# Turning the first two pairs of B·x as plain halves (ScalarE and accumulating transfers), with the fourth chunk's sum of v on the tensor engine

## The chip, the cores and the metric

The kernel runs on one core of a Trainium2 chip. Its time is the device time of one execution in microseconds; runs are summarized by their median. In the text PE is the tensor engine (matmuls), PEld its loading of weights, DVE the vector engine, ACT the scalar engine, POOL GpSimd and SP the sync engine, which issues most transfers.

## The reference

Two branches over a sequence of 2048 rows with 1024 channels, mixed by a gate for each row. Branch a is a diagonal state space model with 1024 complex states; branch b is a short convolution, a product and a long convolution (by FFT) for each channel.

```python
g = sigmoid((x * gate_w).sum(-1, keepdims=True))

# a: h_t = Lam_bar * h_(t-1) + B_bar x_t, complex
Lam_bar = exp(dt * Lam)
B_bar = ((Lam_bar - 1.0) / Lam)[:, None] * Bmat
Bu = einsum("bld,pd->blp", x, B_bar)
h = Lam_bar * h + Bu[:, t]            # for each t
a = 2.0 * einsum("blp,dp->bld", hseq, Cmat).real + x * Dskip

# b: taps of k, times v, long convolution with ssm_k
k_shift = sum over t of k_pad[:, t:t + S] * shift_k[:, 3 - t]
kv = k_shift * v
y = irfft(rfft(kv, 2 S) * rfft(ssm_k, 2 S))[:, :S] + kv * ssm_D
b = x * y

return g * a + (1 - g) * b
```

## The kernel before

**Branch b** is the convolution stage, up to about 210 us. It takes the channels in eight chunks of 128. The FFT is a product with cosine and sine tables (`CF`, `SF`, `NCF` forwards, `CI`, `SI` backwards) on PE. One pass of the main loop, `for c in range(NC - 1)` (lines 1186 to 1312), works on several chunks at once: on DVE the products of the spectra of chunk c (`products`: `acc<-BT,Vh`, `wkh<-BT,Vh` and the sums behind them, at the end `Vh<-acc`); on PE the inverse of chunk c−1 (`inverse`, `psz`, evicted to `cv`), the forward transforms of chunk n = c+1 (`fwd_K`, `psk`, evicted into `BT`; `fwd_V`, `psv`, evicted into `Vh`), and the taps of chunk c+2. ACT evicts nearly all of these. The products of a chunk need all four `Vh` evictions of `fwd_V`, which stand at the end of the pass before.

Before `fwd_V`, the product kv of the chunk has to be folded into two halves (`times_v`, lines 601 to 615): DVE multiplies `ks` by v; PE mirrors `ks` with a reversal matrix (`mirror`), ACT evicts that to `lo`; DVE takes the difference `ev = ks − lo`, and the sum `ks + lo` is made in place by an accumulating transfer issued by GpSimd (`ks<-lo`, the helper `gather`, line 126). The call for chunk c in `times_v(c)` runs in the pass before the one of its products: `times_v(3)` is stepped in pass c=2.

**Branch a** takes time in four blocks of 512 steps (`tb`) and the states in eight groups (`g`) of two times 128, and each pair (tb, g) has two parts j of 128 states. A block's columns are taken in two halves, even and odd steps, and two steps are joined to one: what has to be scanned is V(t) = even(t) + Lam_bar·odd(t−1), complex; this is called turning. `Bu(i)` (lines 833 to 861) makes the i-th pair of `order`. Before the change there are two ways to turn:

- `Bu_tile` (863 to 884), for i = 0 and 1, which are (tb 0, g 0) and (tb 0, g 1): `odd` is evicted to `U`; then PE adds Lam_bar·odd into the PSUM tile `even` by matmuls with diagonal matrices (`even<-U,lamd`, four for each part), and ACT evicts the turned `even`. The diagonals `lamd` are made by `lam_diag` (820 to 831): for g 0 by six scalings on ACT (line 1248), for g 1 by six on DVE at the end of pass c=1 (line 1311).
- `Bu_halves` (888 to 904, i = 2 and 3) and `Bu_plain` (906 to 920, later ones): `even` and `odd` are evicted plainly, into `V_` and `O_`, and `turn_U` (922 to 936) does the rest, in two steps. Step 1: two ACT scalings of 512 columns, `O_` by the real part of lam, into a buffer `Q`, and an accumulating transfer of 256 KB, `U<-Q`. Step 2: four scalings of 256 columns by the imaginary part and its negative, and another such transfer.

The parts of the first four pairs are stepped in between the work of the convolution, at places chosen by hand (`step(parts)`); the turns of pairs 2 and 3 run at lines 1254 and 1364. The scans over the turned pairs (`scan`) and the products with C (`psy`) follow the convolution, from about 208 us to the end.

**The order of the work.** Nothing is reordered: `put` (line 86 and on) chains every instruction behind the one issued before on the same engine, so the order in which the Python code runs is the order on each engine, GpSimd's and SP's queues too. All PSUM tiles come from one pool of four buffers in rotation (`ps2`), so each new tile waits for the eviction of the fourth one before it. `u4` is a pool of three buffers, for `hr`, `t` and `Q`.

All operations go through these helpers, so the trace names the helper's line (L94), and instructions are told apart by their tiles.

## Time and profile before

| | us |
|---|---|
| median of 3 runs (lowest, highest) | 380.2 (378.99, 381.24) |
| the profiled execution | 381.04 |
| its span in the trace | 379.3 |

| engine | busy us | share of the span | instructions |
|---|---|---|---|
| PE | 369.9 | 98% | 2434 |
| PEld | 200.3 | 53% | 2469 |
| DVE | 364.1 | 96% | 585 |
| ACT | 307.6 | 81% | 473 |
| POOL | 79.1 | 21% | 109 |

The span is the time from the first instruction to the last in the trace, the profiled execution's own time lies 1.7 us above it. Busy is the time in which an engine worked on at least one instruction. In the timeline a row has the start, the duration, the engine, the operation with its output and inputs and their shapes, a count when several of one kind follow each other, and in brackets the time for which the engine stood idle ahead of it and what ended that. Since matmuls are pipelined, the duration of one is longer than the step from it to the next.

### The profile page before, as it was taken

What the parts mean: (1) busy time and instruction counts of PE and PEld (TensorE: products, weight loads), DVE (VectorE), ACT (ScalarE), POOL (GpSimd) and SP (SyncE); (2) the same over time, 40 slices, a digit from 0 to 9 for tenths busy, and PEclk for the clock granted to TensorE, in tenths of its full rate; (3) what the DMA queues carried; (4) which work ended last, traced back from release to release, by engine and by line L of the source; (5) the groups of instructions that cost most, each with busy time, mean ns of one, the idle gap of its engine ahead of it and who ended that gap; (6) DMA issues with size and microseconds to landing.
All of it is one profiled execution on the core that took longest, in us unless ns stands there. A gap on an engine that the chain in (4) does not pass through costs nothing.

```text
span 379.3 us, 6647 instructions
## 1 busy us (share of the span) xinstructions
PE 369.9 (98%) x2434; PEld 200.3 (53%) x2469; DVE 364.1 (96%) x585; ACT 307.6 (81%) x473; POOL 79.1 (21%) x109
## 2 busy tenths in 40 slices
PE   7999999999999999999999999989999999999996
PEld 4656467575674847644544444434445444444444
DVE  8899999999999999999999999999999989969984
ACT  5879998988979899697949799998879868938501
POOL 4011030110301102021002012123443313635000
PEclk9999999999999999999999999999999999999999
DMA  7889999999999989968999999947998999998902
GB/s 168 168 114 264 215 213 189 236 218 203 228 200 185 215 166 194 179 145 153 207 183 209 215 186 253 256 101 131 197 247 138 251 247 204 160 255 146 221 0 111
DMA packets 126259, 71.78 MB, mean 189 GB/s; under 512 B 104649, under 2 KB 107601, under 8 KB 126226
## 3 DMA queue, kind: packets, MB, share of 16 engines
q1 hardware_dynamic: 112416, 45.90, 56.1%
q0 software_dynamic: 12688, 25.17, 38.7%
q10 hardware_dynamic: 1122, 0.28, 0.4%
q8 instruction: 19, 0.31, 0.3%
q14 instruction: 14, 0.11, 0.1%
HBM read 15.48 MB, written 8.39 MB: 63 GB/s over the span
## 4 chain that ended last, share of the span: by engine, by line
DVE 55%; PE 26%; issue 8%; DMA 5%; ACT 4%; POOL 0%; SPq 0%; POOLq 0%; DVEq 0%
PE psy L94 23%; DVE acc L94 20%; DVE wkh L94 13%; DVE A L94 5%; DVE Vh L94 4%; DVE t L94 3%; DVE U L94 2%; DVE ks L94 2%; DMA U<-Q 2%; ACT Q L94 2%; DVE trn L94 2%; PE taps L94 1%; DMA kT<-in_B_k_dram 1%; DMA BT<-gd 1%; DVE CT L94 1%
## 5 line engine op out<-in xcount | busy, mean ns | idle before, releaser
L94 PE MATMUL psy<-CT,U 128*128 128x512 bf16 (+1 forms) x418 | 92.7, 374 | 0.4
L94 PEld LDWEIGHTS <-U 128*128 128x128 bf16 x492 | 48.0, 98 | 57.3 <-issue 2.1
L94 PEld LDWEIGHTS <-BT 128*128 128x128 bf16 x544 | 50.5, 98 | 33.5 <-issue 0.2
L94 DVE TENSOR_TENSOR wkh<-BT,Vh 128x2048 bf16<-128x2048 bf16 (+3 forms) x31 | 44.6, 1457 | 0.0
L94 ACT ACTIVATE Q<-U,lam 128x512 bf16<-128x512 bf16 (+1 forms) x64 | 37.5, 632 | 8.5 <-DVE U L94 8.5
L94 POOL DMA_DIRECT2D U<-Q x26 | 26.6, 1033 | 82.9 <-ACT Q L94 42.4
L94 DVE TENSOR_TENSOR acc<-BT,Vh 128x4096 bf16<-128x4096 bf16 (+3 forms) x19 | 36.9, 1947 | 0.3 <-ACT Vh L94 0.2
L94 PE MATMUL both<-xT,BT 128*128 128x512 bf16 x157 | 35.2, 379 | 0.2
L94 ACT ACTIVATE Vh<-psv 128x1024 bf16<-128x1024 f32 x32 | 30.7, 1034 | 5.7 <-PE psv L94 5.6
L94 DVE TENSOR_TENSOR_SCAN A<-rv,init,A 128x256 bf16<-128x256 f32 x48 | 34.4, 738 | 0.0
L94 DVE TENSOR_TENSOR acc<-acc,wkh 128x1024 bf16<-128x1024 bf16 (+4 forms) x30 | 32.7, 1128 | 0.1
L94 ACT ACTIVATE U<-both 128x512 bf16<-128x512 f32 x44 | 24.2, 594 | 10.4 <-PE both L94 10.1
L94 ACT ACTIVATE BT<-psk 128x1024 bf16<-128x1024 f32 x31 | 30.0, 1035 | 2.3 <-PE psk L94 2.2
L94 POOL DMA_DIRECT2D acc<-wkh x8 | 9.7, 1218 | 100.7 <-DVE wkh L94 100.7
L94 PE MATMUL psk<-eok,SF 128*128 128x384 bf16 (+1 forms) x118 | 28.0, 354 | 0.2
L94 PEld LDWEIGHTS <-SF 128*128 128x128 bf16 x184 | 18.0, 98 | 19.1 <-issue 0.4
L94 PE MATMUL psz<-Vh,CI 128*128 128x512 bf16 x64 | 24.3, 379 | 0.0
L94 PE MATMUL psz<-Vh,SI 128*128 128x512 bf16 x64 | 24.3, 379 | 0.0
L94 PE MATMUL taps<-dg,kT 128*128 128x128 bf16 (+1 forms) x352 | 21.5, 208 | 1.0 <-DMA kT<-in_B_k_dram 1.0
L94 PEld LDWEIGHTS <-kT 128*128 128x128 bf16 x352 | 20.8, 99 | 2.5 <-DMA kT<-in_B_k_dram 2.0
L94 DVE TENSOR_TENSOR U<-U,trn 128x512 bf16<-128x512 bf16 (+1 forms) x58 | 21.2, 391 | 0.1
L94 PE MATMUL both<-xT,BTl 128*128 128x512 bf16 x94 | 21.1, 379 | 0.1
(223 smaller groups left out, 767.5 us busy)
## 6 DMA issues: line engine op xcount, KB each, us to landing
U<-Q POOLq DMA_DIRECT2D x26, 256.0 KB, 5.4
acc<-wkh POOLq DMA_DIRECT2D x6, 768.0 KB, 8.7
cv_scr<-cv SPq DMA_DIRECT2D x16, 256.0 KB, 4.8
kn<-in_B_ssm_k_dram SPq DMA_DIRECT2D x5, 512.0 KB, 3.7
v<-in_B_v_dram SPq DMA_DIRECT2D x5, 512.0 KB, 5.9
out_dram<-m SPq DMA_DIRECT2D x8, 256.0 KB, 4.8
BT<-cv_scr SPq DMA_DIRECT2D x7, 256.0 KB, 7.0
out_dram<-BT SPq DMA_DIRECT2D x7, 256.0 KB, 2.0
```

The lines of the kernel that those rows point to most:

```text
L94: i = f(*a, **kw)
```

## The change

The first two pairs are made as the later ones: `Bu_tile` and `lam_diag` go, and pairs 0 and 1 use `Bu_halves`, with `even` and `odd` evicted plainly. Their turns (`turn_U`) run in the passes c=4 (pair 0) and c=5 (pair 1): step 1 behind `fwd_K`, step 2 between the first two and the last two tiles of `fwd_V`. The column before the first step of the first block is set to zero by a small ACT operation (`before_first`). So per pair six ACT scalings and two accumulating transfers of 256 KB come in, and the matmuls with diagonals and the twelve scalings that make the diagonals go.

Besides, the difference `ev = ks − lo` of chunk 3 (stepped in pass c=2) is no longer made by DVE but by PE, in a PSUM tile `whole`: the identity times the upper half of `ks`, plus `refl[:, 0]`, the reversal matrix with the other sign, times the lower; four matmuls of 512 columns, and an ACT eviction.

```diff
@@ kernel's pools
+    s5p["Q"] = s5p["wu"]
...
@@ times_v(c)
         e = eo_pool.tile([128, 2, 4, 128], BF16, name="ev")
-        tt(e, ks[:, 2:4], lo, ALU.subtract)
+        if c == 3:
+            ps = ps2([128, 2, 4, 128], "whole")
+            for mt in range(2):
+                mm(ps[:, mt], ident, ks[:, 2 + mt], True, False)
+                mm(ps[:, mt], refl[:, 0], ks[:, 1 - mt], False, True)
+            act(e, ps, func=ACT.Copy)
+        else:
+            tt(e, ks[:, 2:4], lo, ALU.subtract)
...
-    def lam_diag(g, home, on_act=False):
...
@@ Bu(i)
-        if i >= 2:
-            V_, O_ = U[:, 0:4 * HB], U[:, 4 * HB:]
...
-        U = U[:, 0:8 * HB].rearrange("p (a c j t) -> p a c j t", a=2, c=2, j=2)
-        Us[tb, g] = U[:, 0], U[:, 1]
-        return [Bu_tile(tb, g, U, j) for j in range(2)]
-
-    def Bu_tile(tb, g, U, j):
...
+        V_, O_ = U[:, 0:4 * HB], U[:, 4 * HB:]
+        V_ = V_.rearrange("p (c j t) -> p c j t", c=2, j=2)
+        O_ = O_.rearrange("p (c j t) -> p c j t", c=2, j=2)
+        Us[tb, g] = V_, O_[:, :, :, 2:]
+        turns_U[i] = turn_U(g, V_, O_)
+        return [(Bu_halves if i < 4 else Bu_plain)(tb, g, V_, O_, j) for j in range(2)]
...
+    def before_first(tb, g, O_, j):
+        if j == 0 and tb > 0:
+            act(O_[:, :, :, 1], ends[:, 1 - tb % 2, g], func=ACT.Copy)
+        elif j == 0:
+            act(O_[:, :, :, 1], lam[:, :, 0:2], func=ACT.Copy, scale=0.0)
...
@@ for c in range(NC - 1)
         fwd_K(n, (2, 3))
-        if c == 1:
-            lam_diag(0, lam_pool, True)
         if c == 4:
             step(parts)
+        if c in (4, 5):
+            step(turns_U[c - 4])
         if c == 6:
             run(sp)
-            s5p["Q"] = s5p["wu"]
             run(turns_U[2])
...
         fwd_V(n, (0, 1))
+        if c in (4, 5):
+            run(turns_U[c - 4])
         if c < 6 and c != 4:
             step(parts)
...
         fwd_V(n, (2, 3))
         if c in (4, 5):
             step(parts)
-        if c == 1:
-            lam_diag(1, lam_pool)
```

More of the change, by code (lines that the diff above doesn't have):

```diff
@@ L408 @@
     mlam = small("mlam")
-    lamd = {}
     TCS = rot_pool.tile([128, 2, NP, HB], BF16, name="TCS")
@@ L818 @@
     ends = consts.tile([128, 2, NG, 2, 2], BF16, name="ends")
-    def lam_diag(g, home, on_act=False):
-        if g == 0:
-            lamd["all"] = home.tile([128, 2, 2, 3, 128], BF16, name="lamd", tag="lamd")
-        t = lamd[g] = lamd["all"][:, g]
-        for j in range(2):
-            for k, f in enumerate((lam[:, 0], lam[:, 1], mlam)):
-                pi = 2 * g + j
-                if on_act:
-                    act(t[:, j, k], ident, func=ACT.Identity, scale=f[:, pi:pi + 1])
-                else:
-                    ts(t[:, j, k], ident, f[:, pi:pi + 1], None, ALU.mult)
     def Bu(i):
@@ L851, in Bu @@
                 U = home.tile(shape, BF16, name="U")
-        if i >= 2:
-            V_, O_ = U[:, 0:4 * HB], U[:, 4 * HB:]
-            V_ = V_.rearrange("p (c j t) -> p c j t", c=2, j=2)
-            O_ = O_.rearrange("p (c j t) -> p c j t", c=2, j=2)
-            Us[tb, g] = V_, O_[:, :, :, 2:]
-            turns_U[i] = turn_U(g, V_, O_)
-            return [(Bu_halves if i < 4 else Bu_plain)(tb, g, V_, O_, j) for j in range(2)]
-        U = U[:, 0:8 * HB].rearrange("p (a c j t) -> p a c j t", a=2, c=2, j=2)
@@ L860, in Bu @@
-        Us[tb, g] = U[:, 0], U[:, 1]
-        return [Bu_tile(tb, g, U, j) for j in range(2)]
-    def Bu_tile(tb, g, U, j):
-        xT = xTs[tb]
-        ps = []
-        d = lamd[g][:, j]
-        for a in (1, 0):
-            ps.append(ps2([128, 2, HB], ("even", "odd")[a]))
-            for c in range(2):
-                for dt_ in range(ND):
-                    mm(ps[1 - a][:, c], B_of[g, c][:, dt_, j * 128:(j + 1) * 128], xT[:, dt_, a * HB:(a + 1) * HB],
-                       dt_ == 0 and (a == 1 or c == 0), a == 1 and dt_ == ND - 1)
-            if a == 1:
-                act(U[:, 1, :, j], ps[0], func=ACT.Copy)
-                if j == 1 and tb < NTB - 1:
-                    act(ends[:, tb % 2, g], U[:, 1, :, :, HB - 1], func=ACT.Copy)
-                yield
-        yield
-        for k, c, o in ((0, 0, 0), (0, 1, 1), (1, 0, 1), (2, 1, 0)):
-            if tb > 0:
-                mm(ps[1][:, o, 0:1], d[:, k], ends[:, 1 - tb % 2, g, c, j:j + 1], False, False)
-            mm(ps[1][:, o, 1:HB], d[:, k], U[:, 1, c, j, 0:HB - 1], False, k == 2)
-        act(U[:, 0, :, j], ps[1], func=ACT.Copy)
-        yield
@@ L888, in Bu_halves @@
     def Bu_halves(tb, g, V_, O_, j):
-        if j == 0:
-            act(O_[:, :, :, 1], ends[:, 1 - tb % 2, g], func=ACT.Copy)
+        before_first(tb, g, O_, j)
         for a in (1, 0):
@@ L907, in Bu_plain @@
         xT = xTs[tb]
-        if j == 0 and tb > 0:
-            act(O_[:, :, :, 1], ends[:, 1 - tb % 2, g], func=ACT.Copy)
-        elif j == 0:
-            act(O_[:, :, :, 1], lam[:, :, 0:2], func=ACT.Copy, scale=0.0)
+        before_first(tb, g, O_, j)
         ps = ps2([128, 2, 2, HB], "both")
```

## The prediction

> **What bounds the kernel now.** I read the page first: its busy shares and its chain.

> ```profile
> PE 369.9 (98%) x2434; PEld 200.3 (53%) x2469; DVE 364.1 (96%) x585; ACT 307.6 (81%) x473; POOL 79.1 (21%) x109
> DVE 55%; PE 26%; issue 8%; DMA 5%; ACT 4%; POOL 0%; SPq 0%; POOLq 0%; DVEq 0%
> ```

> Two engines are nearly full, and the chain goes over both. So a microsecond taken from one of them counts only as far as the other, and the hand-overs between them, let it. The next view is the table of stretches for the convolution chunk in which the new transfers begin (c=4, 117 to 140) and the one behind it (columns: span, then busy PE, PEld, DVE, ACT, POOL, clock, DMA share, GB/s).

> ```profile
> 117.00:140.00 23.00, 22.89 (x197) 14.70 (x197) 22.97 (x21) 21.35 (x34) 3.09 (x4) 1.00 1.05 192
> 140.00:163.00 23.00, 22.57 (x195) 14.69 (x196) 22.97 (x21) 18.08 (x28) 3.25 (x4) 1.00 0.93 175
> ```

> PE and DVE leave 0.1 us and less open in c=4; ACT has 1.65 us open there and 4.9 us in c=5. The granted clock is 1.00. So the sum has to be made at the hand-overs, from the timelines of the engines. First DVE: each chunk's products begin with `acc<-BT,Vh` (columns: start, duration).

> ```profile
> 65.09 2.36 DVE L94 TENSOR_TENSOR Vh<-acc 128x2048 bf16<-128x2048 bf16 x2
> ...
> 68.51 0.41 DVE L94 TENSOR_SCALAR lamd<-ident,lam 128x128 bf16<-128x128 bf16 x2
> ...
> 69.48 2.28 DVE L94 TENSOR_TENSOR acc<-BT,Vh 128x4096 bf16<-128x4096 bf16 x1
> ...
> 77.22 0.68 DVE L94 TENSOR_TENSOR ev<-ks,lo 128x1024 bf16<-128x1024 bf16 x1
> 77.83 1.75 DVE L94 TENSOR_TENSOR acc<-acc,wkh 128x3072 bf16<-128x3072 bf16 x1
> ...
> 92.25 2.28 DVE L94 TENSOR_TENSOR acc<-BT,Vh 128x4096 bf16<-128x4096 bf16 x1
> 115.01 2.28 DVE L94 TENSOR_TENSOR acc<-BT,Vh 128x4096 bf16<-128x4096 bf16 x1
> 137.77 2.28 DVE L94 TENSOR_TENSOR acc<-BT,Vh 128x4096 bf16<-128x4096 bf16 x1
> 145.51 0.68 DVE L94 TENSOR_TENSOR ev<-ks,lo 128x1024 bf16<-128x1024 bf16 x1
> 161.13 2.28 DVE L94 TENSOR_TENSOR acc<-BT,Vh 128x4096 bf16<-128x4096 bf16 x1
> ```

> A chunk is 22.76 us of DVE (92.25 to 115.01 to 137.77). Each `acc` needs the four evictions of `Vh` that ACT makes at the end of the chunk before. PE, in turn:

> ```profile
> 66.64 0.38 PE L94 MATMUL psz<-Vh,CI 128*128 128x512 bf16 x1
> ...
> 70.10 0.38 PE L94 MATMUL mirror<-ks,refl 128*128 128x512 bf16 x1
> 70.53 1.91 PE L94 MATMUL even<-xT,BT 128*128 128x256 bf16 x16
> ...
> 75.30 0.60 PE L94 MATMUL even<-U,lamd 128*128 128x255 bf16 x4
> 75.74 0.59 PE L94 MATMUL psk<-eok,CF 128*128 128x512 bf16 x2
> ...
> 152.89 0.59 PE L94 MATMUL psv<-ks,SF 128*128 128x512 bf16 x2 [0.37 <-DMA ks<-lo]
> ...
> 250.32 1.02 PE L94 MATMUL psy<-CTa,U 128*128 128x512 bf16 x4 [1.51 <-ACT U L94]
> ```

> Sixteen `psz` take 3.46 us (66.64 to 70.10), 0.216 us each for 512 columns, one behind the other. The two waits in brackets are the ones that matter behind 150 us: at 152.89 PE stands for the gather `ks<-lo`, and from there on it has no other wait in the convolution. The last rows are ACT's evictions and scalings.

> ```profile
> 65.98 1.94 ACT L94 ACTIVATE Vh<-psv 128x1024 bf16<-128x1024 f32 x2
> ...
> 71.06 1.91 ACT L94 ACTIVATE cv<-psz 128x1024 bf16<-128x1024 f32 x2
> 72.86 1.02 ACT L94 ACTIVATE lo<-mirror 128x1024 bf16<-128x1024 f32 x1
> ...
> 89.56 1.96 ACT L94 ACTIVATE Vh<-psv 128x1024 bf16<-128x1024 f32 x2
> ...
> 129.27 0.60 ACT L94 ACTIVATE U<-odd 128x512 bf16<-128x512 f32 x1 [0.63 <-PE odd L94]
> ...
> 132.89 0.60 ACT L94 ACTIVATE U<-even 128x512 bf16<-128x512 f32 x1 [0.63 <-PE even L94]
> 133.75 3.77 ACT L94 ACTIVATE Vh<-psv 128x1024 bf16<-128x1024 f32 x4 [0.27 <-PE psv L94]
> ...
> 153.51 3.77 ACT L94 ACTIVATE Vh<-psv 128x1024 bf16<-128x1024 f32 x4 [0.58 <-PE psv L94]
> ...
> 182.74 1.77 ACT L94 ACTIVATE Q<-U,lam 128x512 bf16<-128x512 bf16 x3
> 184.36 0.54 ACT L94 ACTIVATE Q<-U,mlam 128x256 bf16<-128x256 bf16 x1
> ...
> 185.56 0.62 ACT L94 ACTIVATE U<-both 128x512 bf16<-128x512 f32 x1
> ```

> The last `Vh` of c=4 is out at 133.75+3.77 = 137.52, and DVE takes it at 137.77: 0.25 us of room. In c=5 it is out at 157.28 and taken at 161.13: 3.85 us of room. That difference carries the forecast.

> **Removed and added work, chunk by chunk.** The profiled execution took 381.04 us (span 379.3 and 1.74 around it); the median of the runs is 380.2, 0.84 below. Shifts are against the trace; minus is earlier.

> *Start of c=2.* The six `lamd` of DVE go: 69.48−68.51 = 0.97 us, and since the last `Vh` was out at 65.98+1.94 = 67.92, `acc` can begin at 68.51. DVE stands at −0.97. ACT's six `lamd` of c=1 go too; ACT waits for PE later in that chunk, so this is worth nothing. PE loses a group of four diagonals near the end of c=1: 75.74−75.30 = 0.44 us by the like group in c=2. Of this only 0.27 is kept, since `psz` at 66.64 needs the first half of DVE's `Vh`, ready half of 2.36 and a little behind 65.09 (66.37 by the like point of the pairs). PE stands at −0.27.

> *The sum of v on PE, in c=2.* DVE loses `ev<-ks,lo`: 77.83−77.22 = 0.61, so −1.58. PE gains four matmuls of 512 columns, 4×0.216 = 0.86. ACT gains one eviction of 128x1024, 72.86 less the middle of the two before it, 0.90 us, behind `lo`; queued behind it are the `dg` scalings, `lo<-kn` and the evictions of `psk`, for which PE's buffers wait. PSUM has four buffers in rotation, and `whole` takes one more: the next tile, `even` (70.53), now has to wait until the first `cv` is out, where it had a free buffer. PE arrives there at 70.53−0.27+0.86 = 71.12. The first `cv` is out half through its row, 71.06+0.98 = 72.04, less 0.44 since ACT's `Vh` at 65.98 follows PE: 71.6. So PE stands about 0.45 longer. Bounds: 0 (ACT is earlier by more) to 0.9 (not earlier). PE: −0.27+0.86+0.45 = +1.04, and two groups of diagonals in c=2 go, 2×0.44: +0.2 at the end of c=2.

> *End of c=2.* The last `Vh` was out at 89.56+1.96 = 91.52; PE's +0.2 to +0.27 moves it to 91.75. DVE comes to its `acc` at 92.25−1.58 = 90.67 and waits. So DVE starts c=3 at 91.79, −0.46: of the 1.58 us taken from DVE 1.1 are gone, since the four `whole` and the buffer hold PE.

> *c=3.* One group of diagonals goes: PE +0.23−0.44 = −0.2. DVE keeps −0.46 (it would take the last `Vh` at 114.55; the evictions, on PE's clock, are out about there).

> *c=4, the first pair's transfers.* Six scalings, by the rows at 182.74 to 185.56: three in 1.62 (two of 512 and one of 256 columns), then 0.40 each, so step 1 (two of 512) is 1.22 us and step 2 (four of 256) 1.60 us. Step 1 stands ahead of the `eok` evictions; behind it ACT waits 0.63, 0.63 and 0.27 for PE up to 133.75, together 1.53, which hide it. Without that cover it would add its 1.22. Step 2 stands between the second and the third `Vh`. There nothing covers it, because the four evictions run back to back (3.77 for four). So the last `Vh` comes out at 137.52−0.2+1.60 = 138.92. DVE would take it at 137.77−0.46 = 137.31, and now waits 1.6 us; behind that wait stands all of c=5 on DVE. DVE starts c=5 at 138.92: **+1.15**.

> *c=5.* PE's stall at 152.89 hangs on DVE, as GpSimd's queue shows.

> ```profile
> 123.73 0.90 POOL L94 DMA_DIRECT2D ks<-lo  x1 [3.27 <-DVE ev L94]
> ...
> 142.01 1.20 POOL L94 DMA_DIRECT2D acc<-wkh  x1 [14.97 <-DVE wkh L94]
> 146.49 0.90 POOL L94 DMA_DIRECT2D ks<-lo  x1 [3.27 <-PE psk L94]
> ```

> The gather `ks<-lo` is issued 0.30 us behind the end of DVE's `ev` (145.51+0.68 = 146.19 to 146.49; one chunk before, where `ev` itself is named, GpSimd's wait has the same 3.27). The page names PE here, but DVE ends last. So the issue moves with DVE by 1.15, and with it the landing and PE's `psv`, from 152.89 to 154.04. PE, at −0.2, would be there at 152.89−0.37−0.2 = 152.3 and waits 1.7 us. From then on PE is at +1.15, too. The second pair's 2.82 us of ACT find 3.85+0.37 us of room ahead of DVE's `acc` at 161.13, and cost nothing; without that room they would be another 1.6.

> *To the end.* From c=5 on neither engine has open time to give back: `psv` to `psy` at 250.32 runs without a wait of PE, and that one waits for ACT, which follows PE's `both`. The shift of **+1.15** reaches the end.

> *The new transfers.* Four gathers of 256 KB more on queue q0; what such cost is in two rows of the page and in one of the DMA's slices, for 142 to 150 us (40 slices of 0.2 us, in tenths).

> ```profile
> q0 software_dynamic: 12688, 25.17, 38.7%
> U<-Q POOLq DMA_DIRECT2D x26, 256.0 KB, 5.4
> DMA  0000007798994799999999998999999999999897
> ```

> q0 moved 25.17 MB in 38.7% of 379.3 us, 5.83 us a MB, so a gather is 0.262 MB or 1.53 us of all sixteen engines. The second one of c=4 is issued at about 137.3, 0.1 behind step 2, and lands some 5.4 us later; what it pushes back finds the idle stretch from 142 to 143.2, 1.2 us, ahead of `acc<-wkh`, which itself now comes 1.15 later. Nothing waits for the turned tiles until the scans, far behind. Bounds: 0, and 1.53 if all of it lands on `ks<-lo`. I take 0.1, nearest the idle stretch. On GpSimd the first gather stands ahead of the `memset` for `kT` of the next chunk, a chunk before it is needed: nothing. SP's queue keeps its order.

> *The sum.* +1.15+0.1 = **+1.25**: 382.3 us for an execution like the profiled one, **381.5** against the median. The unknowns of this case: the buffer stall (0 to 0.9) cancels, because DVE and PE are reset by the `Vh` in c=4; the sum moves with PE's −0.2 there, which would be −0.65 without the stall and +0.25 with a full one; and with the length of step 2. With 0 for the gathers at the lower end and half of one (0.77) at the upper, that is 1.15−0.45 and 1.15+0.45+0.77: 380.9 to 382.6 as this case's own range.

> **The rivals.**

> *The taken work counts (no new wait).* If step 2 doesn't hold the last `Vh` (ACT being far enough ahead, or the scalings running into slack of PE), DVE comes to c=5 at −0.46, and if `whole` doesn't hold PE either, at its full −1.58. Then `ks<-lo` is early, PE's 0.37 goes, and the end moves by between −0.5 and −1.58: 379.7 down to 378.6. For it: DVE has no wait in c=4 (22.97 of 23.00), so what is taken there was on the path. Against it: 3.77 for four evictions leaves no space for 1.60. [...]

> *A gather in the way (slower).* The place is q0 between 137 and 154 us. If the second gather of c=4, or the first one of c=5, is still moving when `ks<-lo` is issued, that gather is 1.53 us later, PE's stall with it, and 1.15+1.53 = +2.7; with both +4.2. That gives 382.9 to 384.4. It decides if `ks<-lo` takes over 6.4+0.8 us from issue to landing (it took 152.84−146.49 = 6.35 or so, PE's wait ending at 152.89). For it: all sixteen engines are at nine tenths from 143.2 to 150. Against it: the idle stretch ahead of that, and the order of the issues (the first gather of c=5 stands behind `ks<-lo`). [...]

> *Nothing moves.* The steps of ACT find room and DVE's saving is lost in the waits for `Vh`: the end stays within 0.4 of 380.2.

> **How the numbers follow.** Chances: the forecast 0.48, the taken work counts 0.24, a gather in the way 0.22, nothing moves 0.06. What a measurement here can tell from no change is about 0.5%, 1.9 us: below 378.3 is faster, above 382.1 slower. The forecast's own range lies above 382.1 for about 0.3 of it, the gathers' case nearly whole (0.22); so slower is 0.14+0.22 = 0.36. The gain's case reaches 378.6, and with the runs' own spread (378.99 to 381.24, 1.1 to each side) about half of it may come out below 378.3: 0.13. The rest, 0.51, is no change to be told. The range takes in the gain's lower end with that spread in part, and most of the gathers' case: 378.2 to 384.0.

> **What would show it.** Right, if in the trace of the changed kernel `acc<-BT,Vh` of c=2 begins about 1 us earlier, that of c=3 about 0.5 earlier after a wait for ACT, and that of c=5 at about 138.9 after a wait of 1.6 for `Vh`, with four `Q` of 256 columns ahead of the last two evictions; if PE waits 1.7 for `ks<-lo` at about 154; and if the spans from there to the end equal those of before. Wrong, if DVE has no such wait at the start of c=5; if `ks<-lo` takes over 7 us to land; or if PE meets a new wait behind 154, at a tile that the sum doesn't name.

## The result and the profile after

| | kernel before | changed kernel |
|---|---|---|
| median, us (8 runs each; lowest, highest) | 380.18 (378.99, 381.24) | 383.9 (381.06, 389.43) |
| ratio to before, 95% interval | | 1.0093 (1.0068 to 1.0117) |
| the profiled execution, its span, its mean granted clock | 381.04, 379.3, 1.00 | 385.08, 383.3, 0.994 |

The changed kernel is 0.9% slower: 3.5 us at 380. Runs of one kernel that a disturbance lengthened as a whole are left out of the ratios here and below. What remains of the changed kernel falls into two groups: three runs with a mean granted clock of 0.999 or more took 381.06, 382.46 and 382.56 us, four with 0.994 to 0.996 took 383.6 to 386.44.

The page after: the two busy lines have hardly moved, but the chain has gone from DVE to PE.

```profile
PE 374.0 (98%) x2457; PEld 200.4 (52%) x2457; DVE 363.4 (95%) x578; ACT 313.3 (82%) x482; POOL 82.3 (21%) x113
PE 75%; DMA 7%; DVE 7%; issue 6%; ACT 3%; POOL 1%; SPq 0%; POOLq 0%; ACTq 0%
```

DVE's timeline after, the starts of the chunks' products c=2 to c=6:

```profile
69.34 2.29 DVE L95 TENSOR_TENSOR acc<-BT,Vh 128x4096 bf16<-128x4096 bf16 x1 [0.83 <-ACT Vh L95]
...
93.59 2.29 DVE L95 TENSOR_TENSOR acc<-BT,Vh 128x4096 bf16<-128x4096 bf16 x1 [1.80 <-ACT Vh L95]
...
116.36 2.29 DVE L95 TENSOR_TENSOR acc<-BT,Vh 128x4096 bf16<-128x4096 bf16 x1
...
140.73 2.29 DVE L95 TENSOR_TENSOR acc<-BT,Vh 128x4096 bf16<-128x4096 bf16 x1 [1.53 <-ACT Vh L95]
...
164.10 2.29 DVE L95 TENSOR_TENSOR acc<-BT,Vh 128x4096 bf16<-128x4096 bf16 x1
```

Three of five starts now wait for ACT's last `Vh`; before, none did. Against before the five stand at −0.14, +1.34, +1.35, +2.96 and +2.97 us. ACT's timeline shows the wait of 1.53 in the making: the four scalings of step 2 stand between the evictions, 1.59 us from the first to the next `Vh`.

```profile
137.18 0.51 ACT L95 ACTIVATE Q<-U,lam 128x256 bf16<-128x256 bf16 x1
...
138.77 1.93 ACT L95 ACTIVATE Vh<-psv 128x1024 bf16<-128x1024 f32 x2
```

PE's timeline after, its waits, and what follows the last of them:

```profile
56.62 1.91 PE L95 MATMUL odd<-xT,BT 128*128 128x256 bf16 x16 [0.90 <-DMA xT<-in_A_x_dram]
...
59.18 0.23 PE L95 MATMUL taps<-dg,kT 128*128 128x64 bf16 x2 [0.65 <-DMA kT<-kT]
...
73.50 1.91 PE L95 MATMUL even<-xT,BT 128*128 128x256 bf16 x16 [0.56 <-ACT cv L95]
...
156.84 0.87 PE L95 MATMUL psv<-ks,SF 128*128 128x512 bf16 x2 [2.35 <-DMA ks<-lo]
157.50 1.06 PE L95 MATMUL psv<-ev,CF 128*128 128x512 bf16 x2
...
161.55 1.91 PE L95 MATMUL odd<-xT,BT 128*128 128x256 bf16 x16
...
254.36 0.81 PE L95 MATMUL psy<-CTa,U 128*128 128x512 bf16 x3
```

The wait of 0.56 is the buffer stall of the sum on PE. The two waits at 56 and 59 us, in c=1, are for loads, ahead of most of the change. Behind the wait of 2.35 a pair of 512-column matmuls takes 1.06 instead of 0.59. The table of windows shows why (the third figure from the right is the granted clock):

```profile
156.00:157.00 1.00, 0.16 (x1) 0.10 (x1) 1.00 (x2) 0.00 (x0) 0.00 (x0) 1.00 1.00 130
157.00:158.00 1.00, 1.00 (x4) 0.37 (x3) 1.00 (x3) 0.25 (x1) 0.00 (x0) 0.51 1.13 205
...
160.00:161.00 1.00, 1.00 (x5) 0.44 (x4) 0.97 (x2) 1.00 (x3) 0.00 (x0) 0.78 2.05 155
161.00:162.00 1.00, 1.00 (x9) 0.60 (x8) 1.00 (x2) 1.00 (x4) 0.00 (x0) 1.00 0.84 74
```

PE's clock fell to half for over 3 us after it had stood still. From `psv<-ks` to `odd` it took 161.55−156.84 = 4.71 us; without a fall, in the second trace of the same kernel below, 158.47−155.45 = 3.02. So the fall costs 1.7 us. Before, the same `odd` stands here:

```profile
155.90 1.91 PE L94 MATMUL odd<-xT,BT 128*128 128x256 bf16 x16
```

The profiled difference, 385.08−381.04 = 4.04 us, adds up along the chain: +1.35 that DVE brings into c=4 (the two waits for loads in c=1, 1.55 us, are in it, and whether they belong to the change stays open), +1.61 at its start of c=5, +0.99 that `ks<-lo` takes longer (PE's `psv` at 156.84, +3.95), +1.70 by the clock (`odd` at 161.55 against 155.90, +5.65), −1.61 up to `psy`, since PE's wait of 1.51 ahead of it has gone (254.36 against 250.32, +4.04).

### The profile page after: what moved, and what is told of

The parts are those of the page before. It is cut to its first block, busy times and chain, and to the rows that moved or that the text cites. A ratio compares the mean times of both kernels' runs of the same rounds, so it can differ in the third digit from the quotient of the medians.

```text
span 383.3 us, 6668 instructions
## 1 busy us (share of the span) xinstructions
PE 374.0 (98%) x2457; PEld 200.4 (52%) x2457; DVE 363.4 (95%) x578; ACT 313.3 (82%) x482; POOL 82.3 (21%) x113
## 4 chain that ended last, share of the span: by engine, by line
PE 75%; DMA 7%; DVE 7%; issue 6%; ACT 3%; POOL 1%; SPq 0%; POOLq 0%; ACTq 0%
PE psy L95 29%; PE both L95 22%; PE psk L95 6%; PE psv L95 5%; PE taps L95 4%; PE psz L95 4%; DVE acc L95 3%; DVE wkh L95 3%; PE foldk L95 2%; DMA kT<-kT 2%; DMA ks<-lo 2%; PE even L95 2%; ACT Vh L95 1%; PE odd L95 1%; DMA U<-Q 1%
## 5 line engine op out<-in xcount | busy, mean ns | idle before, releaser
L95 POOL DMA_DIRECT2D U<-Q x30 | 29.8, 1005 | 105.7 <-ACT Q L95 48.7
L95 ACT ACTIVATE Q<-U,lam 128x512 bf16<-128x512 bf16 (+1 forms) x72 | 42.3, 632 | 6.8 <-issue 3.4
L95 ACT ACTIVATE U<-both 128x512 bf16<-128x512 f32 x44 | 24.2, 594 | 10.4 <-PE both L95 10.1
L95 PEld LDWEIGHTS <-kT 128*128 128x128 bf16 x352 | 21.6, 101 | 2.4 <-DMA kT<-in_B_k_dram 1.1
L95 PE MATMUL psv<-ks,SF 128*128 128x512 bf16 x64 | 20.0, 395 | 2.3 <-DMA ks<-lo 2.3
## 6 DMA issues: line engine op xcount, KB each, us to landing
U<-Q POOLq DMA_DIRECT2D x30, 256.0 KB, 4.7
cv_scr<-cv SPq DMA_DIRECT2D x16, 256.0 KB, 5.4
out_dram<-m SPq DMA_DIRECT2D x8, 256.0 KB, 4.6
BT<-cv_scr SPq DMA_DIRECT2D x7, 256.0 KB, 7.9
out_dram<-BT SPq DMA_DIRECT2D x7, 256.0 KB, 2.0
```

Source lines behind the costliest of these rows:

```text
L95: i = f(*a, **kw)
```

## The experiments

All ratios are to the kernel before, run in the same group on the same chip. "Falls" counts the runs with a mean granted clock under 0.998, of those that enter the ratio.

| label | what is different | ratio (95% interval) | falls |
|---|---|---|---|
| r_after_again | the changed kernel once more, the control | 1.0092 (1.0057 to 1.0128) | 5 of 6 |
| e1_sum_only | only the sum on PE | 1.0020 (0.9991 to 1.0049) | 0 of 10 |
| e2_turns_only | only the turns | 1.0036 (0.9996 to 1.0076) | 4 of 9 |
| e3_step2_behind | step 2 behind fwd_V | 1.0052 (1.0009 to 1.0095) | 5 of 10 |
| e4_fill | fill at ks<-lo | 1.0106 (1.0054 to 1.0158) | 3 of 5 |
| e5_no_transfers | no transfers of pairs 0, 1 | 1.0032 (1.0007 to 1.0057) | 0 of 10 |
| e7_fill_taps | e3, and fill at the taps | 1.0101 (1.0068 to 1.0135) | 1 of 6 |
| e8_bound | all costs found taken out | 0.9987 (0.9955 to 1.0018) | 0 of 10 |
| e6_late, r_late_again | turns late in c=5, no sum on PE | 1.0020 (0.9982 to 1.0058), 1.0136 (1.0088 to 1.0184) | 1 of 5, 3 of 3 |

**The sum on PE alone**: the kernel before with this edit.

```diff
         e = eo_pool.tile([128, 2, 4, 128], BF16, name="ev")
-        tt(e, ks[:, 2:4], lo, ALU.subtract)
+        if c == 3: ...  (four matmuls into "whole", an ACT eviction)
+        else: tt(e, ks[:, 2:4], lo, ALU.subtract)
```

> The kernel before with the fourth chunk's sum of v on PE alone (no change to the first two pairs). If the four matmuls and the eviction hold PE in c=2, as the sum has it: a wait of PE for the eviction of cv of about 0.5 us, the last Vh of c=2 about 1.3 us later than before, DVE's acc of c=3 about +0.6 us, and the end at +0.6 to +1.0 us (380.8 to 381.2), with no fall of PE's clock. If the loss of the change lies in the turns or their transfers alone: within 0.3 us of before. If DVE's 0.6 us counted: 379.6.

PE's timeline and DVE's, from c=2 on:

```profile
71.89 1.91 PE L94 MATMUL even<-xT,BT 128*128 128x256 bf16 x16 [0.56 <-ACT cv L94]
```

```profile
92.91 2.29 DVE L94 TENSOR_TENSOR acc<-BT,Vh 128x4096 bf16<-128x4096 bf16 x1 [1.23 <-ACT Vh L94]
```

The stall is there with the 0.5 us expected, and DVE's 0.61 us come back as a wait of 1.23: c=3 begins 0.66 later than before. The ratio, 0.2%, has 1 inside its interval. So the sum on PE gives nothing that can be told; that it costs is shown in the trace, not in the time.

**The turns alone**: the changed kernel, with the difference of chunk 3 made by DVE again.

> The changed kernel without the sum on PE: the chunk-3 difference is DVE's again. If step 2 between the evictions of Vh is the cause: DVE comes to c=4 about 1.0 us ahead of before, waits 1.4 us or so for the last Vh at the start of c=5 and stands there at +0.4 to +0.6 us; PE's wait for ks<-lo is about 2 us; the end is 380.6 to 381 where PE's clock stays, 1.5 us more where it falls to half behind that wait. If the transfers' share of the DMA engines is the cause: 382.5 or more, and ks<-lo takes over 7 us from its issue to PE's start.

The expected place was not where this trace lost its time. DVE waits only 0.34 us there and begins c=5 0.59 us earlier than before: step 2's four scalings (1.59 us in the profiled run) stand between the evictions here too, but PE had begun its `psv` 1.96 us earlier than before (130.73 against 132.69). PE waits at another place:

```profile
137.18 2.29 DVE L95 TENSOR_TENSOR acc<-BT,Vh 128x4096 bf16<-128x4096 bf16 x1 [0.34 <-ACT Vh L95]
```

```profile
150.43 0.27 PE L95 MATMUL taps<-dg,kT 128*128 128x64 bf16 x2 [3.53 <-DMA kT<-kT]
```

(This execution took 388.83 us. PE also stands 4.46 us in it at 221.61, which no other trace shows; only the taps, which come in e3, e4 and e7 too, are read here.) These are the taps made in c=5, and what is late is the keys: `kT` is loaded and transposed from memory (SP), copied to `kB`, then partly overwritten by `kT<-kT`, each behind the landing of the one before (SP stands 0.4 us for the landing of `kT` and 3.3 for that of `kB` in before, 0.2 and 3.8 in the profiled run of the changed kernel). SP's timeline of this kernel and of before:

```profile
130.56 4.50 SPq L95 DMA_TRANSPOSE kT<-in_B_k_dram  x1
...
144.29 0.46 SPq L95 DMA_DIRECT2D kT<-kT  x1
```

```profile
132.28 1.94 SPq L94 DMA_TRANSPOSE kT<-in_B_k_dram  x1
...
142.22 0.46 SPq L94 DMA_DIRECT2D kT<-kT  x1
```

From the one issue to the other it is 13.73 us with the two new transfers of c=4 beside it, and 9.94 without. In the profiled run of the changed kernel it is 11.40, and PE didn't wait at these taps:

```profile
134.11 3.23 SPq L95 DMA_TRANSPOSE kT<-in_B_k_dram  x1
...
145.51 0.46 SPq L95 DMA_DIRECT2D kT<-kT  x1
```

**Step 2 behind the last Vh.**

```diff
         fwd_V(n, (0, 1))
-        if c in (4, 5):
-            run(turns_U[c - 4])
...
         fwd_V(n, (2, 3))
         if c in (4, 5):
+            run(turns_U[c - 4])
             step(parts)
```

> The changed kernel with step 2 of both turns (four scalings and the transfer) moved behind the last tiles of fwd_V, so that no scaling stands between evictions of Vh. If step 2's place is the cause: no wait of DVE at the start of c=5 over 0.3 us, PE's wait for ks<-lo under 1 us, its clock at 1.00 throughout, and 380 to 381.5 us. If the transfers are the cause, they are all still there, about 1.5 us later: 383 to 384 us as before.

DVE starts c=5 without a wait; PE's new wait is at the taps again, and the clock falls behind it (`even`, sixteen in 2.92 us instead of 1.91):

```profile
137.54 2.28 DVE L95 TENSOR_TENSOR acc<-BT,Vh 128x4096 bf16<-128x4096 bf16 x1
```

```profile
150.93 0.22 PE L95 MATMUL taps<-dg,kT 128*128 128x64 bf16 x2 [2.50 <-ACT U L95]
...
153.47 2.92 PE L95 MATMUL even<-xT,BT 128*128 128x256 bf16 x16
...
156.22 0.38 PE L95 MATMUL psv<-ev,CF 128*128 128x512 bf16 x1
```

The page names ACT here. In e2 and e7 the same wait ends with `kT<-kT`, 6.14 and 6.04 us behind its issue (144.29 and 146.97); here these taps begin 5.18 us behind it (145.75), in e4 7.43 (144.11). That the keys end the wait in e3 and e4 too is an inference from this, not shown by a row. The wait of DVE behind step 2 is caused by its place, but it isn't the whole loss: with it gone the ratio is still 1.0052, above 1 with its whole interval. That interval overlaps the changed kernel's, so what the move gains in time is not shown. Each of the two causes that the expectation names, the place and the transfers, holds a part.

**A fill where PE stood for `ks<-lo`.**

```diff
             for cc in range(2):
+                for k in range(10 if c == 6 and fi == 0 and cc == 1 else 0):
+                    mm(ps[:, 1], CF[:, 0, fsl], eo[0][:, 0], True, True)
```

> The changed kernel with ten more matmuls of 512 columns (2.2 us, into a half of the PSUM tile that is overwritten afterwards) in the place where PE stands for ks<-lo in c=5. If the fall of the clock behind that wait costs time: the mean clock is 1.00 in every run, the wait shrinks to 0.3 us or nothing, and the time is 1 to 2 us under the changed kernel's (382 to 383 us, and less spread). If it only goes with the wait and costs nothing at the end: 383.9 us as before.

It missed: in this trace PE stood at the taps ahead of the fill, so that the fill was only more work. It tells nothing of what a fall of the clock costs.

```profile
151.54 0.22 PE L95 MATMUL taps<-dg,kT 128*128 128x64 bf16 x2 [3.17 <-ACT U L95]
```

Up to this row e4 issues the same work as the changed kernel, so the wait at the taps comes in that kernel too, though in neither of its own two traces.

**The control, and the transfers left out.**

> The changed kernel unaltered, as the control of this group. If its loss has two waits that take turns (DVE for the last Vh at the start of c=5, and PE for the keys' kT or for ks<-lo at 150 to 157 us), this trace shows at least one of 1.5 us or more; PE's waits for transfers at 56 to 59 us come back only if they belong to the change. Time 383 to 385 us.

```diff
-            gather(V_, Q)
+            if moves:          # False for pairs 0 and 1
+                gather(V_, Q)
             yield
```

> The changed kernel without the four accumulating transfers of pairs 0 and 1 (their scalings stay, so those two pairs are not turned). If the wait for the last Vh behind step 2 is all: the transfers cost nothing, 383 to 384 us as the changed kernel. If the transfers on the shared engines delay the keys' kT and ks<-lo: the issue of kT<-kT is back at 142 to 143.5 us and PE doesn't wait for it, ks<-lo takes 6.4 us again, PE's one wait there is 1.7 us, and the time is the forecast's own 381 to 382 us.

The control's trace is of its one run without a fall of the clock, 381.98 us. Its DVE and PE, then the same without the transfers:

```profile
91.43 2.29 DVE L95 TENSOR_TENSOR acc<-BT,Vh 128x4096 bf16<-128x4096 bf16 x1 [0.83 <-ACT Vh L95]
...
139.96 2.29 DVE L95 TENSOR_TENSOR acc<-BT,Vh 128x4096 bf16<-128x4096 bf16 x1 [2.35 <-ACT Vh L95]
```

```profile
124.34 1.92 PE L95 MATMUL even<-xT,BT 128*128 128x256 bf16 x16 [1.31 <-DMA xT<-in_A_x_dram]
...
155.45 0.59 PE L95 MATMUL psv<-ks,SF 128*128 128x512 bf16 x2 [1.94 <-DMA ks<-lo]
...
158.47 1.91 PE L95 MATMUL odd<-xT,BT 128*128 128x256 bf16 x16
```

```profile
140.15 2.29 DVE L95 TENSOR_TENSOR acc<-BT,Vh 128x4096 bf16<-128x4096 bf16 x1 [1.53 <-ACT Vh L95]
```

```profile
155.33 0.59 PE L95 MATMUL psv<-ks,SF 128*128 128x512 bf16 x2 [1.63 <-DMA ks<-lo]
...
251.93 1.02 PE L95 MATMUL psy<-CTa,U 128*128 128x512 bf16 x4 [0.68 <-ACT U L95]
```

```profile
133.52 2.60 SPq L95 DMA_TRANSPOSE kT<-in_B_k_dram  x1
...
144.07 0.46 SPq L95 DMA_DIRECT2D kT<-kT  x1
```

Without the transfers all twelve scalings stay, and the wait of 1.53 too, and the time is the forecast's own: 1.0032 against 381.5/380.2 = 1.0034. With them it is 1.0092. The transfers are worth 0.6%, 2.3 us at 380; the two intervals touch at 1.0057, and the first measurement of the changed kernel (from 1.0068) lies above. The way from `kT` to `kT<-kT` tells the same without the noise of the time: 10.55 us here, 9.84 in e1, 10.3 in e8 (below), 10.4 in a second trace of the kernel before, 9.7 to 9.9 where the turns come later; with the transfers in c=4 it is 11.4 (changed kernel), 11.6 (control), 12.1 (e4), 13.7, 13.7 and 13.8 (e2, e3, e7). And the clock fell in none of the 20 runs of e1 and e5, but in 22 of the 43 with transfers in c=4, the fill at the taps included. The experiment leaves out all four transfers, those of c=5 too; which of them costs how much is not shown.

**A fill at the taps**, in e3's kernel.

```diff
         ps = ps2([128, 8, 128], "taps")
+        for n in range(10 if fill and h == 0 else 0):     # c == 7
+            mm(ps[:, 0:4], CF[:, 0, 0:128], CF[:, 0], True, True)
```

> The kernel with step 2 behind fwd_V (e3_step2_behind), and ten more matmuls of 512 columns (2.2 us, in a region that is overwritten afterwards) ahead of the taps of c=5, where PE waited 2.5 us for the keys. If the fall of PE's clock behind such a wait is what makes the runs over 383 us: PE's wait there is under 1 us, the mean clock 0.998 or more, and the undisturbed runs lie at 381 to 382.5 us. If the clock is without effect on the end: 383 to 385 us in half the runs, as without the fill.

```profile
153.01 0.22 PE L95 MATMUL taps<-dg,kT 128*128 128x64 bf16 x2 [1.34 <-DMA kT<-kT]
...
156.68 0.38 PE L95 MATMUL psv<-ev,CF 128*128 128x512 bf16 x1
```

The clock stays (1.00 in four of six runs, one under 0.998), and the same work from the taps to `psv` takes 156.68−153.01 = 3.67 us, against 156.22−150.93 = 5.29 in e3: a fall costs 1.6 us, as above. But the time didn't get better. The keys came still later here (`kT<-kT` is issued at 146.97, in e3 at 145.75), so that fill and wait together, 3.5 us, were longer than e3's 2.50. Five of the six runs kept a clock of 0.999 or more and took 383.41 to 386.51 us, so the fall of the clock alone doesn't make the runs over 383 us. What the standing costs by itself this kernel can't tell, since the fill is work of its own.

**Taken out together.** e2's sum, e3's place and e5's missing transfers in one kernel.

> What is left when both costs found so far are taken out: the changed kernel without the sum on PE, with step 2 behind fwd_V, and without the four transfers of pairs 0 and 1 (those two pairs are not turned; all scalings stay). If the loss is the sum on PE, step 2's place and the transfers, and nothing else: DVE comes to c=5 about 0.8 to 1.0 us ahead of before without a wait, PE's wait for ks<-lo is 0.4 us, its clock 0.998 or more, and the time is 379.2 to 379.8 against 380.2, the 0.97 us that the diagonals took from DVE. If the scalings on ACT or the evictions cost more than the rows show: 380.5 us or more.

```profile
124.25 1.92 PE L95 MATMUL even<-xT,BT 128*128 128x256 bf16 x16 [1.95 <-DMA xT<-in_A_x_dram]
```

```profile
138.30 2.29 DVE L95 TENSOR_TENSOR acc<-BT,Vh 128x4096 bf16<-128x4096 bf16 x1 [1.28 <-ACT Vh L95]
```

```profile
249.31 1.02 PE L95 MATMUL psy<-CTa,U 128*128 128x512 bf16 x4
```

The ratio is 0.9987 with 1 inside: no loss is left, and no gain that can be told. DVE came to c=4 at 114.18, 0.83 ahead of before; but PE, ahead as well, then stood 1.95 us for the second block's xT, and through `Vh` DVE lost what it had and began c=5 0.53 us later than before. The end came earlier all the same: `psy` stands at 249.31 without a wait, 1.01 ahead of before, and this execution took 380.02 us against 381.04. The expected 379.2 to 379.8 against 380.2 is a ratio of 0.9974 to 0.9989; 0.9987 lies in it, but the interval reaches from a gain larger than that to no gain, so whether DVE's 0.97 us counted stays open.

**Both turns late, two tries at a version that gains.**

```diff
+        if c == 5:
+            step(turns_U[0])
         fwd_V(n, (0, 1))
+        if c == 5:
+            run(turns_U[0])
...
         fwd_V(n, (2, 3))
+        if c == 5:
+            run(turns_U[1])
```

> The changed kernel with the difference of chunk 3 back on DVE and both turns late in c=5: step 1 of pair 0 ahead of fwd_V, its step 2 between the tiles, both steps of pair 1 behind them. The room there is 3.9 us of ACT ahead of DVE's acc, and c=5 loads no keys. If step 2's place in c=4 and the transfers' collision with the keys are the whole loss: no wait of DVE at the start of c=5, PE's wait for ks<-lo under 0.6 us, and DVE's 0.97 us for the diagonals count: 379 to 380 us against 380.2. If the turning costs wherever it stands (ACT or the transfers of c=5): 381 us or more.

> The kernel with both turns late in c=5 (e6_late) once more, for a second trace: its runs lay between 379.2 and 390 us, while the trace was of one of the best. If xT's load, which is moving while the new transfers are issued at 153 to 162 us, is what comes late in the others: PE waits 2 us or more for xT at 166 to 168 us, and its clock falls behind that. If it is something else, the wait stands elsewhere.

The first trace was of a run of 379.23 us and shows what was hoped for: DVE at c=5 at 137.00 without a wait, PE's wait for `ks<-lo` 0.37. Nine of the twelve runs were longer, 383 us and over. The second trace shows no wait at xT behind 160 us, but one behind it, for the next B, whose load took 7.99 us of issue (2.95 in before):

```profile
181.29 7.99 SPq L95 DMA_TRANSPOSE BT<-in_A_B_im_dram  x1
```

```profile
194.61 7.04 PE L95 MATMUL both<-xT,BT 128*128 128x512 bf16 x24 [2.49 <-DMA BT<-in_A_B_im_dram]
...
243.71 10.02 PE L95 MATMUL both<-xT,BTl 128*128 128x512 bf16 x32 [10.99 <-ACT U L95]
```

That execution took 402.09 us, though, and its longest wait, 10.99 us, stands in no other trace, so it doesn't tell why the other runs were long.

> A try at a version that gains: no sum on PE, pair 0 turned at the end of c=5, its transfers held behind the landing of xT (GpSimd's stamp goes ahead of them), where all transfers pause at 162 to 167 us in the trace of before; pair 1 turned in the last chunk behind the gates. If the loss was the collision of the transfers with the transposed loads of keys and xT: no wait of PE over 0.6 us up to 190 us, 379.3 to 380 us. If each such transfer costs wherever it stands, since the later stretches are as full: 381 us or more, with a wait of PE or ACT for a load behind 190 us.

In the trace of before the DMA share from 162 to 167 us is 0.00, 0.70, 0.05, 0.64 and 0.00, us by us: pauses with two bursts between them. This kernel gave 383.29 us at the best and up to 401.87. In its trace, of a run of 385.61 us, PE waits for the same load:

```profile
194.00 5.35 PE L95 MATMUL both<-xT,BT 128*128 128x512 bf16 x24 [2.61 <-DMA BT<-in_A_B_im_dram]
```

The load of B is longer in both traces (4.13 us of issue here, 7.99 in the other, 2.95 in before); that it is what lengthens the other runs is not shown. Neither try beats the kernel before. A second trace of the kernel before was taken to see whether the waits for loads of c=1 and at 124 us come in it, too:

> The kernel before, unaltered, for a second trace of it. If PE's waits for loads at 56 to 59 us (xT, keys) and at 124 us (xT) that some traces of the changed kernels show are a wobble of the loads in any execution, this trace may show one; if they belong to the change, it shows none, as the first one. ks<-lo of c=5 takes 6.4 us, PE's wait for it is 0.4 us, the clock is 0.998 or more, 379 to 382 us.

It shows none of them up to 160 us; that execution took 388.26 us, with waits behind 228 us that the first trace of this kernel doesn't show, so nothing more is read from it. Those at 56 to 59 us are in four of the traces of changed kernels with 0.6 us or more, e5 and e6 among them, and not in the control. Whether they belong to the change stays open.

## Why the prediction was right, and where it was not

The direction was right and 383.9 is inside the range, near its upper end; it is 2.4 us above the forecast of 381.5. It also lies above the 380.9 to 382.6 that the sum itself allowed, among the 382.9 to 384.4 of the rival of a gather in the way. So the sum gave the direction, and the number is inside only because the range was drawn to take in that rival.

- **By the signs that the prediction named**, the traces are mixed. In the profiled run c=2 begins 0.14 us earlier, not 1, c=3 begins 1.34 later, not 0.5 earlier, and `ks<-lo` takes over 7 us, which was a sign of being wrong. In the control c=2 begins at 68.16, 1.32 earlier, c=3 0.82 earlier and c=5 at 139.96 after a wait of 2.35, with PE's wait of 1.31 for xT ahead of it.
- **The sum on PE, buffer stall 0.45 us, bounds 0 to 0.9**: 0.39 to 0.56 in the traces that have the sum. DVE's gain lost at the end of c=2: forecast a wait of 1.1, the control 0.83. In the profiled run it was 1.80, since PE had already lost 0.90 and 0.65 to loads.
- **Step 2 between the evictions, wait of 1.6 us, DVE at +1.15**: 1.53 or 1.54 in the changed kernel, in e4 and in e5. Its cause is shown by e3, where moving step 2 removes it. Its size depends on where PE stands: 2.35 in the control, behind PE's wait for xT, and 0.34 in e2, where PE was about 2 us ahead. The start of c=5 was at +2.96 and +2.19 in the two traces of the changed kernel and at −0.59 in e2.
- **PE's wait for `ks<-lo`, 1.7 us**: 1.63 in e5, where the new transfers are left out.
- **The new transfers, 0.1 us: the term that was mis-sized.** It measures 0.6%, 2.3 us. The sum looked at the idle stretch from 142 us and at `ks<-lo`, which took 7.37 us from issue to PE's start in the profiled run and 6.76 in the control, against 6.40 (6.45 in e5, but 6.82 in e1, which has none of the new transfers; in the control and in e5 the issue is put 0.30 us behind the end of DVE's `ev`, as in before). It said of the keys only that SP's queue keeps its order. That order was kept; but the transposed load of the keys became longer (3.23 us of issue in the profiled run against 1.94), and the chain of three that ends at the taps had no room: PE waited 2.5 to 3.5 us there in e2, e3 and e4, though not in the two traces of the changed kernel itself. This is the rival's mechanism at another place than the rival named. How the 2.3 us divide between the keys, `ks<-lo` and the clock is not shown. With GpSimd's new transfers in c=4, SP's chain of the keys was 1.5 to 3.9 us longer than its 9.9 in the kernel before (9.7 to 10.6 in all traces without them in c=4).
- **"From c=5 on neither engine has open time to give back"**: wrong. The wait of 1.51 us ahead of `psy` was not ACT following PE. ACT's timeline, before and after, shows it standing for a transfer, `U<-Q`, and after that for less:

```profile
212.57 0.22 ACT L94 ACTIVATE U<-ends 128x4 bf16<-128x4 bf16 x1 [2.51 <-DMA U<-Q]
```

```profile
216.46 0.22 ACT L95 ACTIVATE U<-ends 128x4 bf16<-128x4 bf16 x1 [0.76 <-DMA U<-Q]
```

  PE's wait went to 0.68 in e5 and to nothing in the changed kernel, and hid that much. So the sum had two errors of opposite sign, the missing transfers the larger. That e5's ratio comes so near to the forecast is in part luck: in its trace DVE stood at +2.38 at c=5, not at +1.15, and PE's shorter wait took 0.83 of it back.
- **Clock**: not in the sum at all. Where it fell behind one of PE's waits, that cost 1.6 to 1.7 us more.
- **The rival that the taken work counts** needs DVE to meet no new wait, and the changed kernel's waits at c=3 and c=5 refute that. Whether work taken from DVE counts by itself is not decided: in e1 the 0.61 us taken from DVE came back as a wait, and in e8, with the costs out, DVE's gain is gone at c=5, while the ratio of 0.9987 (0.9955 to 1.0018) leaves room for the full 0.97 us as well as for none.

## What to carry to other kernels

Where a kernel's loads are themselves a chain (load, copy, overwrite) with its end just in time, price a new transfer by what it does to every step of that chain, not by the queue it is issued on or by its share of the engines: here the sum had 0.1 us for four transfers, and they measured 2.3. Look at a step that is moved in between the evictions of a set as if the set's last reader waited for it in full: here 1.59 us of scalings gave 1.53 of wait, and less (0.34) only where PE was ahead. And before offloading a full engine, ask what load the others reach early: in e8 DVE's lead of 0.83 us was gone behind PE's wait of 1.95 for such a load.

## What was not expected of the hardware

```profile
254.89 1.02 PE L95 MATMUL psy<-CTa,U 128*128 128x512 bf16 x4 [2.82 <-ACT U L95]
```

Worked out from the granted clock, us by us, the half rate lasted 3.4 us in the profiled run (0.51, 0.50, 0.50 and 0.78 from 157 on), in e2 (0.92, 0.50, 0.50, 0.50 and 0.88 from 149 on) and in e3 (0.56, 0.50, 0.50 and 0.73 from 152 on). What sets it off, no run here shows.

The transposed load of the keys, `kT`, took 2.78 to 4.50 us of issue in the six traces with the new transfers in c=4, 1.94 to 2.60 in the eight without. The load of `kn` right behind it shows no such difference: 2.37 to 3.16 us with them, 2.33 to 3.18 without.
